# First two heads' queries from raw tokens, their mean and scale put in behind, in an attention and MLP kernel

## The chip, the cores and the metric

The kernel runs on one core of one Trainium2 chip. Its time is the device time of one execution in microseconds, given as the median of several runs. A profile is one execution recorded by the hardware profiler; its span runs from the first to the last instruction of the program and is a little shorter than the device time of the same execution.

## The reference

One layer with two branches over 2048 tokens of width 512. All inputs are bf16.

```python
x  = A_x                               # 1 x 2048 x 512
xn = layernorm(x)                      # no gain, no bias, eps 1e-5
# attention branch: 32 heads of width 128, keys and values from a cache of 2048 entries
q  = (xn @ wq) split into heads        # wq: 512 x 4096
p  = softmax(q k^T * 128**-0.5)
s  = (p v, heads joined) @ wo          # wo: 4096 x 512
# MLP branch on the same xn
h  = gelu(layernorm(xn) @ w1)
hs = four quarters of h, shifted by +1, -1, +2, -2 tokens, @ w2
x1 = xn + hs
g  = silu(x1 + gelu(layernorm(x1) @ w3) @ w4)
out = x + s * g
```

## The kernel before

The attention branch sets the order. Its work is cut into 128 units: 8 groups of 4 heads, in each group 4 tiles of 512 queries, for each tile the 4 heads. A unit has 8 slots. A slot `n` handles 256 of the 2048 keys: two 128x512 score matmuls into a pair of PSUM banks (`s_slot`, tile `ps_s`, of which there are two), one ScalarE exponential of 128x1024 into `pT`, and two value matmuls into `ps_o` (`pv_slot`) for a slot that lies some slots back. That distance is the lag: 5 at the start, raised by one at each slot number in `STEPS` until it is 12 from slot 158 on. There are 1024 slots. In between VectorE adds up the `pT` tiles (`add_first`, `add_next`, `fold`) for the softmax sums. The sums of the first four units are turned by small matmuls (`sums`), those of later ones by a DMA transposition; the reciprocals go through DRAM and come back on all partitions (`bcast`), and `norm` multiplies the unit's output with them.

The query of a unit (`q_mm`, `q_copy`) is four matmuls over `xnT`, the transposed normalized tokens, into a bank of the pool `psX`. This pool has two tags with one buffer each, "xa" and "xm". A tile with such a tag waits until the earlier tile of the tag has been read. Row sums, output projections (`wo_mm`) and the MLP's matmuls take these two banks as well.

All of it is one program written slot by slot in the loop over `n`. Each engine and each DMA queue (SP's, ACT's, POOL's) executes its own instructions strictly in the program's order; `pin` keeps that order. `at(n, fn)` puts a piece of work behind slot `n`; the table `tokens` holds, for the token tiles 4 to 15, the slots of their statistics, of their normalization and of the transposition into `xnT`. The MLP's chunks start in unit 5.

The start of the program stands ahead of slot 0. Four tiles of 128 tokens are loaded on the SP and ACT queues, the query weights of heads 0 to 3 on the POOL queue, keys (by transposing DMA, `load_k`, four pieces of 512 keys a head) and values (`load_v`, two halves a head) on the SP queue. TensorE does 48 matmuls of no use on the identity (`warm_up`). `first_stats` takes mean and variance of the four tiles (VectorE, one tile on ScalarE) and the factor (variance + eps) to the power -0.5 on GpSimd. `first_tokens` normalizes each tile on VectorE, transposes it by four matmuls with the identity, copies it to `xnT`, and makes head 0's query in pieces of 128 tokens. The queries of heads 1 to 3 follow in slots 1, 3 and 5 and are copied by VectorE in slots 2, 4 and 6.

Of the kernel before, what the change touches and what calls it, by code (L numbers as in the profile page):

```python
# [17 lines left out]
def kernel(  # L18
# [36 lines left out]
    LAG = 5  # L55
# [5 lines left out]
    WARM = 48  # L61
# [3 lines left out]
    def pool(name, bufs=1, space=None, **kw):  # L65
        if space is not None:
# [11 lines left out]
    nc.vector.memset(ones_t[:], 1.0)  # L78
    nc.vector.memset(nhalf[:], -0.5)
    ident = const.tile([P, P], BF16, name="ident")  # L80
    diag = const.tile([P, P], FP32, name="diag")
    pin(nc.gpsimd.iota(diag[:], pattern=[[-1, P]], base=0, channel_multiplier=1,
                       allow_small_or_imprecise_dtypes=True))
    pin(nc.vector.tensor_scalar(
        out=ident[:], in0=diag[:], scalar1=0.0, scalar2=None, op0=ALU.is_equal))
# [20 lines left out]

    xsrc = x2d.rearrange("(t p) d -> t p d", p=P)
    wq_v = A_wq.rearrange("(dc p) j -> p dc j", p=P)
# [34 lines left out]
    STEPS = (36, 40, 44, 48, 49, 150, 158)  # L143
    LAGS = [(n, LAG + i) for i, n in enumerate(STEPS)] + [(NS, LAG + len(STEPS))]
    kTs, vBs, wqs, wos, oTs, st = {}, {}, {}, {}, {}, {}
# [135 lines left out]
    def bcast(u):  # L281
        st[u]["rb"] = (tl["rb"].tile([P, 512], FP32, tag="rb3", bufs=2, name="rb") if u >= T1 else rp.tile([P, 512], FP32, name="rb"))
# [111 lines left out]
    def ln1_load(t, eng):  # L394
        xin = tokp.tile([P, D], BF16, tag="ta", bufs=6, name="xin")
# [10 lines left out]
    def first_stats():  # L406
        root = D ** -0.5
        nm = smp.tile([P, 1], FP32, name="nm")
        junk = gtp.tile([P, D], BF16, tag="pre", name="pre")
        pin(nc.scalar.activation(  # L410
            out=junk[:], in_=ln[3][:], func=ACT.Identity, scale=-root / D, accum_out=nm[:]))
        pin(nc.scalar.activation(
            out=junk[:], in_=ln[3][:], func=ACT.Square, scale=root, bias=nm[:],
            accum_out=mvA[:, 3, 1:2]))
        for t in range(3):
            bn = smp.tile([P, nc.vector.BN_STATS_DIM], FP32, name="bn")
            pin(nc.vector.bn_stats(out=bn[:], in_=ln[t][:]))
            pin(nc.vector.bn_aggr(out=mvA[:, t, :], in_=bn[:]))
        for a, b in ((0, 1), (1, 2), (2, 4)):
            ve = smp.tile([P, b - a], FP32, name="ve")  # L420
            pin(nc.gpsimd.tensor_scalar(
                out=ve[:], in0=mvA[:, a:b, 1], scalar1=EPS, scalar2=None, op0=ALU.add))
            pin(nc.gpsimd.tensor_tensor(
                out=rsA[:, a:b], in0=ve[:], in1=nhalf[:, 0:b - a], op=ALU.pow))
        return lambda: pin(nc.vector.tensor_scalar(
            out=mvA[:, 3, 0:1], in0=nm[:], scalar1=-1.0 / root, scalar2=None, op0=ALU.mult))

# [5 lines left out]
    def ln1_norm(t):  # L433
        xin = ln.pop(t)
        xn = ph1.tile([P, D], BF16, tag="xn", bufs=5, name="xn")
# [11 lines left out]
    def warm_up(n):  # L447
        wt = psS.tile([P, 2, 512], FP32, name="ps_s")
        for _ in range(n):
            mm(wt[:, 0, 0:P], ident[:], ident[:], True, True)  # L450

    def first_tokens():
        xns = [ln1_norm(t) for t in range(2)]
        mean_3()
        xns += [ln1_norm(t) for t in range(2, 4)]
# [552 lines left out]
```

## Time and profile before

| | us |
|---|---|
| median of 3 runs | 1249.34 (1248.23 to 1252.16) |
| the profiled execution | 1248.59 |
| its span | 1246.8 |
| TensorE matmul busy | 1239.2 (99%) |
| VectorE busy | 1115.2 (89%) |
| ScalarE busy | 1129.5 (91%) |
| GpSimd busy | 171.3 (14%) |
| first exponential starts | 10.67 |

A row of the timeline reads: start, length, engine (with a q: its queue issues a DMA), line, operation, output<-inputs by the program's names, shapes, how many instructions the row joins, and in brackets how long the engine had been idle and what ended that. A group of a tile's view gives shortest, median and longest duration in ns, and first and last start. A row of the waits gives who waited for whom, the sum in us, the number and the longest. A row of the windows gives a stretch, its length, then busy time and number of instructions of each engine that the view holds, granted TensorE clock, DMA share and GB/s. A matmul's length in a row contains its way through the array; how often one can start is read from the distance of starts. PE is TensorE, PEld its weight load, DVE VectorE, ACT ScalarE, POOL GpSimd, SP the queue that only issues DMAs.

### The profile page before, as it was taken

What the parts mean: (1) busy time and instruction counts of PE and PEld (TensorE: products, weight loads), DVE (VectorE), ACT (ScalarE), POOL (GpSimd) and SP (SyncE); (2) the same over time, 40 slices, a digit from 0 to 9 for tenths busy, and PEclk for the clock granted to TensorE, in tenths of its full rate; (3) what the DMA queues carried; (4) which work ended last, traced back from release to release, by engine and by line L of the source; (5) the groups of instructions that cost most, each with busy time, mean ns of one, the idle gap of its engine ahead of it and who ended that gap; (6) DMA issues with size and microseconds to landing.
All of it is one profiled execution on the core that took longest, in us unless ns stands there. A gap on an engine that the chain in (4) does not pass through costs nothing.

```text
span 1246.8 us, 16616 instructions
## 1 busy us (share of the span) xinstructions
PE 1239.2 (99%) x5808; PEld 596.4 (48%) x5808; DVE 1115.2 (89%) x1518; ACT 1129.5 (91%) x1285; POOL 171.3 (14%) x299
## 2 busy tenths in 40 slices
PE   8999999999999999999999999999999999999998
PEld 5444444444444444444444444444444444444444
DVE  7999999999899988899989889899888999888998
ACT  8999999888999888899998889998888999988992
POOL 5563003432111000000100000010000000000110
PEclk9999999999999999999999999999999999999999
DMA  9556473565734545243573345633345233653453
GB/s 198 126 111 104 88 154 77 129 130 114 153 67 101 114 98 120 55 88 73 108 155 85 68 76 106 136 79 83 81 105 119 56 89 66 130 136 77 106 149 106
DMA packets 248404, 131.42 MB, mean 105 GB/s; under 512 B 200000, under 2 KB 224960, under 8 KB 248320
## 3 DMA queue, kind: packets, MB, share of 16 engines
q1 hardware_dynamic: 238752, 103.94, 41.1%
q0 software_dynamic: 8992, 25.96, 8.0%
q8 instruction: 45, 0.74, 0.3%
q10 hardware_dynamic: 576, 0.46, 0.1%
q14 instruction: 39, 0.32, 0.1%
HBM read 83.62 MB, written 8.13 MB: 74 GB/s over the span
## 4 chain that ended last, share of the span: by engine, by line
PE 93%; DVE 3%; DMA 2%; ACT 1%; issue 0%; SPq 0%; DVEq 0%
PE ps_s L122 34%; PE ps_o L122 33%; PE ps_m L122 9%; PE ps_wo L122 8%; PE ps_q L122 8%; DMA rb<-dr 1%; DVE acc L224 1%; ACT pT L213 1%; DMA dr<-rc 0%; DVE acc L219 0%; DMA accT<-acc 0%; DVE qT L199 0%; DVE sm L266 0%; DVE acc L228 0%; DVE oT L293 0%
## 5 line engine op out<-in xcount | busy, mean ns | idle before, releaser
L213 ACT ACTIVATE pT<-ps_s 128x1024 bf16<-128x1024 f32 x1024 | 1022.1, 1029 | 90.7 <-PE ps_s L122 76.3
L122 PE MATMUL ps_s<-qT,kT 128*128 128x512 bf16 x2048 | 608.8, 379 | 0.8 <-ACT pT L213 0.5
L122 PE MATMUL ps_o<-pT,vb 128*128 128x512 bf16 x2048 | 607.4, 379 | 0.4 <-DVE oT L300 0.4
L122 PEld LDWEIGHTS <-kT 128*128 128x128 bf16 x2048 | 231.7, 113 | 228.8 <-issue 6.0
L224 DVE TENSOR_TENSOR acc<-acc,pT 128x2048 bf16<-128x2048 bf16 x256 | 308.9, 1207 | 7.3 <-ACT pT L213 6.6
L122 PEld LDWEIGHTS <-vb 128*128 128x128 bf16 x2048 | 200.2, 98 | 226.0 <-issue 0.7
L219 DVE TENSOR_TENSOR acc<-pT 128x2048 bf16<-128x2048 bf16 x128 | 156.2, 1221 | 30.9 <-ACT pT L213 30.5
L122 PE MATMUL ps_q<-xnT,wq_h 128*128 128x512 bf16 (+1 forms) x524 | 152.8, 374 | 0.6 <-ACT xnT L477 0.4
L293 DVE TENSOR_TENSOR oT<-ps_o,rb 128x512 bf16<-128x512 f32 x122 | 130.8, 1072 | 9.5 <-DMA rb<-dr 9.4
L122 PE MATMUL ps_wo<-wo_h,oT 128*128 128x512 bf16 (+1 forms) x460 | 135.1, 377 | 0.0
L379 DVE TENSOR_TENSOR s_acc<-ps_wo,s_acc 128x512 f32<-128x512 f32 x96 | 66.0, 688 | 42.6 <-PE ps_wo L122 42.4
L228 DVE TENSOR_TENSOR acc<-acc 128x1024 bf16<-128x1024 bf16 x128 | 87.5, 683 | 0.9
L266 DVE TENSOR_REDUCE sm<-accT 128x4 f32<-128x512 bf16 x122 | 83.0, 680 | 1.1 <-DMA accT<-acc 1.0
L199 DVE CAST qT<-ps_q 128x512 bf16<-128x512 f32 x109 | 75.0, 688 | 7.9 <-PE ps_q L122 6.9
L122 PEld LDWEIGHTS <-wq_h 128*128 128x128 bf16 x524 | 50.8, 98 | 60.8 <-issue 1.0
L122 PE MATMUL ps_m<-w_sb,h2T 128*128 128x512 bf16 x224 | 77.1, 379 | 0.5 <-DVE xr L700 0.5
L122 PE MATMUL ps_m<-xn2T,w_sb 128*128 128x512 bf16 x224 | 77.1, 379 | 0.0
L682 POOL DMA_DIRECT2D w_sb<-in_B_w_dram x28 | 21.2, 756 | 372.3 <-PE ps_m L122 325.3
L122 PEld LDWEIGHTS <-oT 128*128 128x128 bf16 x468 | 45.7, 98 | 54.1
L710 POOL DMA_DIRECT2D g_d<-xr x16 | 8.8, 548 | 438.3 <-DVE xr L708 438.3
L229 DVE TENSOR_TENSOR acc<-acc 128x512 bf16<-128x512 bf16 x128 | 54.4, 425 | 4.4
L514 DVE SCALAR_TENSOR_TENSOR sq<-sq,pre 128x1024 bf16<-128x1024 bf16 x36 | 44.0, 1222 | 4.7 <-ACT sq L510 4.6
(98 smaller groups left out, 627.9 us busy)
## 6 DMA issues: line engine op xcount, KB each, us to landing
rb<-dr SPq DMA_DIRECT2D x127, 256.0 KB, 3.9
vb<-in_A_v_cache_dram SPq DMA_DIRECT2D x60, 256.0 KB, 3.4
w_sb<-in_B_w_dram POOLq DMA_DIRECT2D x28, 256.0 KB, 3.6
wo_h<-in_A_wo_dram SPq DMA_DIRECT2D x32, 128.0 KB, 2.8
wq_h<-in_A_wq_dram SPq DMA_DIRECT2D x28, 128.0 KB, 2.9
kT<-in_A_k_cache_dram SPq DMA_TRANSPOSE x128, 3.4
dr<-rc SPq DMA_DIRECT2D x128, 2.0 KB, 1.7
xr<-in_A_x_dram POOLq DMA_DIRECT2D x16, 128.0 KB, 2.5
```

The costliest lines, as they stand in the source:

```text
L122: pin(nc.tensor.matmul(out=out, lhsT=lhsT, rhs=rhs, start=start, stop=stop))
L199: pin(nc.vector.tensor_copy(out=qT[:], in_=st[u].pop("psq")[:]))
L213: pin(nc.scalar.activation(out=s["pT"][-1][:, jj:jj + 2, :], in_=sps[:], func=ACT.Exp, scale=SCALE))
L219: pin(nc.vector.tensor_tensor(out=s["acc"][:], in0=s["pT"][0][:], in1=s["pT"][1][:], op=ALU.add))
L224: pin(nc.vector.tensor_tensor(out=a[:], in0=a[:], in1=st[u]["pT"][i][:], op=ALU.add))
L228: pin(nc.vector.tensor_tensor(out=a[:, 0:2, :], in0=a[:, 0:2, :], in1=a[:, 2:4, :], op=ALU.add))
L229: pin(nc.vector.tensor_tensor(out=a[:, 0, :], in0=a[:, 0, :], in1=a[:, 1, :], op=ALU.add))
L266: pin(nc.vector.tensor_reduce(out=sm[:], in_=s.pop("at")[:], axis=mybir.AxisListType.X, op=ALU.add))
L293: pin(nc.vector.tensor_tensor(out=oTs[(g, qt)][:, hh, :].rearrange(f, j=4), in0=s["o"].rearrange(f, j=4), in1=s["rb"].rearrange("x (p j) - ...
L379: pin(nc.vector.tensor_tensor(out=sa, in0=ps[:], in1=sa, op=ALU.add))
L514: pin(nc.vector.scalar_tensor_tensor(out=sq[:].rearrange(f2), in0=sq[:].rearrange(f2), scalar=1.0, in1=pre[:].rearrange(f2), op0=ALU.add, ...
L682: pin(nc.gpsimd.dma_start(out=w[:], in_=w3_v[:, :, fc * P:(fc + 2) * P]))
```

## The change

The query of heads 0 and 1 for the first 512 tokens no longer waits for normalized tokens. The raw tiles are transposed as they land, into `xT`. For head 0, two halves of 256 tokens each, and for head 1 all 512:

- `q_raw`: four matmuls of the query weights with `xT`;
- `q_mean`: one more matmul into the same bank that contracts over a single row, the column sums of the weights (`w_sum`, `w_copy`) with the row of negative token means (`means`, `m_copy`);
- `q_scale`: VectorE multiplies the bank with the tokens' factors, spread over the partitions by matmuls (`factors`; the factor is split into a bf16 part and a bf16 remainder, `high` and `low`) and copied to `rsb` by ScalarE (first half) and VectorE (second half).

Slots 0 and 1 are done in `first_tokens` in halves of 256 queries (`s_part`). The first 512 keys of head 0 are loaded as they are (`kx`, ACT queue), transposed by four matmuls (`k_turn`) and copied by VectorE (`k_back`). `xnT` of the first 512 tokens is made afterwards for heads 2, 3 and the MLP: VectorE adds the mean (`centred`), GpSimd multiplies by the factor (`scaled`), each in four pieces of 128x512. Queries 2 and 3 move to slots 9 and 10, and 13 and 14. The statistics of the first four tiles are all taken by VectorE, in two pairs, with two powers on GpSimd.

Around this: the query weights of heads 0 to 3 come in two loads of two heads; the x tiles 4 to 7 are loaded on SP's queue and normalized in place; the warm-up has 23 matmuls on a tile of constants and does not need the identity; the lag starts at 3; the table of token tiles, the loads of keys and values of heads 2 and 3 and of the output weights, and the slots of row sums, broadcasts and normalizations of the first units are moved; unit 2's value bank is "xm"; queries 5 and 6 are made in two slots with two matmuls each.

```diff
-    LAG = 5
+    LAG = 3
-    WARM = 48
+    WARM = 23
+    CENT, SCAL = (0, 0, 1, 1), (1, 1, 2, 2)
+    FA, FN = ((0, 1), (2,), (3,)), (1, 2)
+    QNEXT = ((2, 9), (3, 13))
...
-    STEPS = (36, 40, 44, 48, 49, 150, 158)
+    STEPS = (14, 25, 33, 41, 44, 48, 49, 150, 158)
...
-            st[u] = dict(psq=psX.tile([P, 512], FP32, tag="xm" if HG <= u < HG + 3 or u > QUIET + 1 else "xa", name="ps_q"))
+            st[u] = dict(psq=psX.tile([P, 512], FP32, tag="xm" if u in (2, 3) or u > QUIET + 1 else "xa", name="ps_q"))
...
-            s["o"] = psO.tile([P, 512], FP32, name="ps_o")
+            s["o"] = (psX.tile([P, 512], FP32, tag="xm", name="ps_o") if u == 2 else
+                      psO.tile([P, 512], FP32, name="ps_o"))
...
+    def q_raw(h, dcs, ps, cs=slice(0, 512), last=False):
+        for dc in dcs:
+            mm(ps[:, cs], wqs[h][:, dc, :], raw["xT"][:, dc, cs], dc == 0, last and dc == DC - 1)
+
+    def q_mean(h, ps, cs=slice(0, 512)):
+        mm(ps[:, cs], raw["ws"][:, h * P:(h + 1) * P], raw["nmb"][0:1, cs], False, True)
+
+    def q_scale(h, ps, rb, cs=slice(0, 512)):
...
+        pin(nc.vector.tensor_tensor(out=st[h]["qT"][:, cs], in0=ps, in1=rb, op=ALU.mult))
...
+        stats(0)
+        for t in range(2):
+            turn(t)
+            back(t)
         turn(2)
...
+        turn(3)
+        back(2)
+        stats(1)
+        means(0)
+        m_copy(0)
...
+        k_turn(kps)
+        w_sum(0, rps[0])
+        w_copy(0, rps[0])
+        back(3)
...
+        q_raw(0, range(DC), psq[0], H2[0])
+        factors(0)
...
+        q_mean(0, psq[0], H2[0])
+        means(1)
+        m_copy(1)
+        q_raw(0, range(DC), psq[1], H2[1])
+        k_back(kps[:])
...
+        q_scale(0, psq[0][:, H2[0]], rsb[:, H2[0]], H2[0])
+        q_mean(0, psq[1], H2[1])
...
+        s_part(0, H2[0])
+        high(1)
+        low(1)
...
+        s_part(1, H2[0])
+        factors(1)
+        q_scale(0, rps[1][:, H2[0]], qs[:], H2[1])
+        q_raw(1, FA[0], raw["ps"])
+        for p in range(2):
+            s_part(p, H2[1])
+        pin(nc.vector.tensor_copy(out=rsb[:, H2[1]], in_=rps[1][:, H2[0]]))
+
+    def centred(dc):
+        pin(nc.vector.tensor_tensor(
+            out=xnT[:, dc, 0:512], in0=raw["xT"][:, dc, :], in1=raw["nmb"][:], op=ALU.add))
+
+    def scaled(dc):
+        pin(nc.gpsimd.tensor_tensor(
+            out=xnT[:, dc, 0:512], in0=xnT[:, dc, 0:512], in1=raw["rb"][:], op=ALU.mult))
...
-    tokens = ((2, 4, 5), (5, 9, 11), (8, 12, 13), (11, 14, 14),
-              (21, 27, 27), (26, 31, 31), (33, 36, 36), (35, 39, 39),
-              (37, 45, 45), (47, 53, 53), (55, 61, 61), (63, 69, 69))
+    tokens = ((2, 5, 6), (4, 7, 8), (7, 11, 12), (9, 13, 14),
+              (16, 20, 20), (21, 25, 25), (29, 35, 35), (34, 38, 38),
+              (49, 55, 55), (55, 61, 61), (60, 66, 66), (65, 70, 70))
...
-        at(3 + i, lambda i=i: load_v(2, (i,), nc.gpsimd))
+        at(7 + i, lambda i=i: load_v(2, (i,), nc.gpsimd))
...
+    norms = {26: 0, 34: 1, 38: 2, 42: 3}
...
-        s_slot(u, p)
+        if n > 1:
+            s_slot(u, p)
...
-        if u == 0 and p in (1, 3, 5):
-            q_mm(1 + p // 2, range(DC))
-        if u == 0 and p in (2, 4, 6):
-            q_copy(p // 2)
+        if n in FN:
+            q_raw(1, FA[1 + FN.index(n)], raw["ps"])
+        if n == FN[-1]:
+            q_mean(1, raw["ps"])
+            q_scale(1, raw["ps"][:], raw["rb"][:])
+        for dc in range(DC):
+            if CENT[dc] == n:
+                centred(dc)
+            if SCAL[dc] == n:
+                scaled(dc)
+        for h, n0 in QNEXT:
+            if n in (n0, n0 + 1):
+                q_mm(h, (2 * (n - n0), 2 * (n - n0) + 1))
+            if n == n0 + 2:
+                q_copy(h)
```

More of the change, by code (lines that the diff above doesn't have):

```diff
@@ L77 @@
     rstd2 = const.tile([P, NT], FP32, name="rstd2")
[L78 to L85, printed above, removed]
     kp = ent(pool("kp", HG + 1))
@@ L404, in ln1_stats @@
         rsqrt(rs1[t][:], mv1[t][:, 1:2])
[L406 to L426, printed above, removed]
     def norm1(t, out, in_):
```

208 lines of the change are left out of this document (141 added, 67 removed).

## The prediction

> **What bounds the kernel now.** I read the page first (busy time, the chain that ended last), then the timeline of the first 40 us, the waits of the first 60 us, and single tiles.
>
> ```profile
> span 1246.8 us, 16616 instructions
> PE 93%; DVE 3%; DMA 2%; ACT 1%; issue 0%; SPq 0%; DVEq 0%
> 1.39 4.33 PE L122 MATMUL ps_s<-ident 128*128 128x128 bf16 x48 [1.39 <-DVE ident L84]
> 3.31 0.69 DVE L417 BATCH_NORM_STATS2 bn<-xin 128x6 f32<-128x512 bf16 x1 [1.98 <-DMA xin<-in_A_x_dram]
> 4.36 0.63 ACT L410 ACTIVATE pre<-xin 128x512 bf16<-128x512 bf16 x1 [1.21 <-DMA xin<-in_A_x_dram]
> 6.17 0.88 PE L122 MATMUL ps_o<-ident,xn 128*128 128x128 bf16 x8 [0.44 <-DVE xn L429]
> 10.04 1.03 PE L122 MATMUL ps_s<-qT,kT 128*128 128x512 bf16 x4 [0.36 <-ACT qT L499]
> 11.77 0.59 PE L122 MATMUL ps_s<-qT,kT 128*128 128x512 bf16 x2
> 16.85 14.77 ACT L213 ACTIVATE pT<-ps_s 128x1024 bf16<-128x1024 f32 x16 [0.33 <-PE ps_s L122]
> 17.95 0.59 PE L122 MATMUL ps_s<-qT,kT 128*128 128x512 bf16 x2
> 18.38 0.59 PE L122 MATMUL ps_o<-pT,vb 128*128 128x512 bf16 x2
> ```
>
> TensorE is the chain: 93%. The last two rows start 0.43 us apart for two matmuls, so one 512-wide matmul costs 0.2155 us; a slot (2 score, 2 value matmuls) costs TensorE 0.86 us. In the early slots ScalarE is just slower: (14.77 - 1.03)/15 = 0.916 us per exponential of 16. A slot with two query matmuls costs 6 x 0.2155 = 1.29 us. From slot 2 on (scores at 11.77) hardly any time is free, so a change ahead of it moves the end by what it moves that start, and every later wait of TensorE adds fully. What can be gained lies ahead of 10 us: the first x tile is there at 3.31, the last of four at 4.36, but the first useful matmul comes at 6.17 and the first scores at 10.04, because statistics, normalization, transposition and queries stand in a row. The profiled execution took 1248.59 us; my sum is made against that. The median of the runs shown is 1249.34, 0.75 higher.
>
> **The start, new.** The rows that price it:
>
> ```profile
> 4.04 0.18 DVE L418 BATCH_NORM_AGGREGATE mvA<-bn 128x2 f32<-128x6 f32 x1
> 4.14 0.66 DVE L417 BATCH_NORM_STATS2 bn<-xin 128x6 f32<-128x512 bf16 x1
> 6.34 0.82 POOL L423 TENSOR_TENSOR rsA<-ve,nhalf 128x2 f32<-128x2 f32 x1
> 6.60 1.09 ACT L477 ACTIVATE xnT<-ps_o 128x512 bf16<-128x512 f32 x2 [0.67 <-PE ps_o L122]
> 8.60 0.38 ACT L494 ACTIVATE qT<-ps_q 128x256 bf16<-128x256 f32 x1
> 14.16 0.69 DVE L199 CAST qT<-ps_q 128x512 bf16<-128x512 f32 x1 [0.64 <-PE ps_q L122]
> L300 DVE TENSOR_TENSOR oT<-ps_o,rb x7: 415/684/692, 30.1 to 1235.4; 128x512 bf16<-128x512 f32 x5, 128x256 bf16<-128x256 f32 x2
> DMA to landing us min/median/max: 4.4/5.3/6.3
> DMA to landing us min/median/max: 4.0/5.7/7.9
> ```
>
> Raw tiles go to TensorE as they land, behind 23 warm-up matmuls (about 1.1 to 3.5 us). ScalarE's four evictions (1.09/2 each) end near 7.1 with the small copies among them. VectorE sets the pace: four statistics of 0.69 from 3.31, some eleven small ones about 0.10 apart, the key eviction of 0.69: 7.85. The factor of the first half (power of 0.82 on GpSimd, hidden behind the second pair of statistics) goes through TensorE and a ScalarE copy of 0.38 and is ready near 7.9. So the first scaled query half takes 7.95 to 8.37 (0.415), the first half scores start at 8.45, the second half is scaled by 9.72, and the four half exponentials (about 0.5 each, from the 0.54 of a 512-wide activation) run from 8.95 to 11.2. Slot 2 needs the PSUM pair of the third of them, which ends near 10.7: its scores start at 10.75, not 11.77: **-1.02**.
>
> The change adds 24 matmuls of 128 columns, 2 of 256 and 1 of 512 to TensorE, 4096 columns, 8 x 0.2155 = 1.7 us. All but the last query matmul of head 1 and its mean row fit into waits ahead of 10.75. Those two are still owed: **+0.43**.
>
> Queues. POOL issues two pairs of wq, the first ahead of the index tile; the identity comes near 2.2, and is first needed at 3.5 (if that cover failed, the same delay would reach the transposes). The wq landing times (4.4 to 6.3 us, first of the two landing rows) put the first pair at 5.3 to 7.1; it is needed near 6.5: I take 0, and 0.5 if late. ACT's queue gets one issue for the raw keys while ScalarE waits for tiles: 0. SP loses one transposing load, gets four x tiles from POOL and sends the first values earlier (near 4.2; by the second landing row, 4.0 to 7.9, there at 8.2 to 12.1). First use is slot 3 at 12.0: 0, at worst 0.1. The 25 dropped warm-ups lay in front of work that waited anyway: 0, unless the clock suffers (below). The shorter lag moves value matmuls forward without changing their number, and by slot 158 both kernels have the same lag: 0.
>
> **What the new work does to VectorE and GpSimd.** The normalized tokens are still needed for heads 2 and 3: four 128x512 sums on VectorE (`centred`) and four 128x512 products on GpSimd (`scaled`). Behind those on POOL stands the factor of token tile 4, and VectorE, in order, waits for it before it applies tile 4. Behind that instruction on VectorE stand the sums of exponentials, statistics of tiles 6 and 7, and then the copy of query 2 that frees the bank "xm". TensorE's query 3 in slot 13 waits for that copy.
>
> ```profile
> 12.60 0.69 DVE L402 BATCH_NORM_STATS2 bn<-xin 128x6 f32<-128x512 bf16 x1
> 13.33 0.18 DVE L403 BATCH_NORM_AGGREGATE mv<-bn 128x2 f32<-128x6 f32 x1
> 13.61 0.22 POOL L126 TENSOR_SCALAR ve<-mv 128x1 f32<-128x1 f32 x1 [2.08 <-DVE mv L403]
> 13.91 0.57 POOL L127 TENSOR_TENSOR rs<-ve,nhalf 128x1 f32<-128x1 f32 x1
> 14.76 1.22 DVE L219 TENSOR_TENSOR acc<-pT 128x2048 bf16<-128x2048 bf16 x1
> 15.90 0.41 DVE L429 TENSOR_SCALAR xn<-xin,mv,rs 128x512 bf16<-128x512 bf16 x1
> 20.19 0.69 DVE L228 TENSOR_TENSOR acc<-acc 128x1024 bf16<-128x1024 bf16 x1
> 20.92 0.43 DVE L229 TENSOR_TENSOR acc<-acc 128x512 bf16<-128x512 bf16 x1
> 22.38 0.18 DVE L251 RECIPROCAL rc<-ps_sum 128x4 f32<-128x4 f32 x1
> 23.27 1.19 DVE L219 TENSOR_TENSOR acc<-pT 128x2048 bf16<-128x2048 bf16 x1
> 23.44 1.10 POOL L126 TENSOR_SCALAR ve<-mv 128x1 f32<-128x1 f32 x1 [0.25 <-DVE mv L403]
> L132 POOL TENSOR_TENSOR vn<-vn,rsA 128x1 f32<-128x1 f32 x4 | 0.9, 235 | 0.3
> PE ps_o L122 <- DVE oT L300: 0.4, 1, 0.4
> PE ps_s L122 <- ACT pT L213: 0.3, 1, 0.3
> ```
>
> No wide GpSimd arithmetic is in this trace. Low end of one product: 0.43, VectorE's own 128x512 sum. I take 0.9: VectorE's 128x512 product with an fp32 factor (0.684) and the 0.2 that a GpSimd product of one column costs; it is the nearest row in kind and size. High end: the row at 23.44 took 1.10 instead of 0.22 because a VectorE sum of two tiles ran from 23.27 to 24.46, so each product may lose another 0.88: 1.78.
>
> VectorE: second half scaled at 9.72, factor copy 10.1, four sums of 0.43 to 11.8, query 1 scaled to 12.5, statistics of tile 4 to 13.4, first sum of exponentials. GpSimd: two products 11.8 to 13.6; the sum of exponentials (1.22) comes in between to 14.85; two more to 16.65; factor of tile 4 (0.22 + 0.57 and gaps, 0.9) to 17.55. VectorE resumes at 17.6: apply 0.41, sum 1.22, apply 0.41, statistics 0.9, sum 1.22, folds 1.15, statistics 0.9, copy 0.69: 6.9, so query 2 is copied at 24.5. TensorE: slot 2 ends 10.75 + 0.86 = 11.61; six slots of 0.916 to 17.1; slots 9 and 10 with 1.29 to 19.7; two more to 21.5; scores and values of slot 13 to 22.4. Query 3 waits from 22.4 to 24.5: **+2.1**. From that copy to the copy of query 4 VectorE has 12.0 us (five sums 6.1, folds 1.15, three applications 1.23, two reciprocals 0.36, two statistics 1.8, two copies 1.38): 36.5. TensorE gets to query 5, which needs that bank, in slot 24 at 24.5 + 0.56 (half a query, row sums) + 0.86 (slot 14) + 7 x 0.916 + 0.13 (row sums) + 2.58 (slots 22 and 23) + 0.86 = 35.9: **+0.6**. GpSimd products themselves end at 16.65, ahead of query 2's second half in slot 10 (near 19): 0. The key loads and transposes behind SP's waits are due with at least a microsecond left. The later normalization of head 0 (slot 26) is due for a value bank in slot 29 with 0.2 us left: 0.
>
> Two waits of before, the 0.4 for a value bank and the 0.3 in the last two rows, stand at places that the change rebuilds (head 2's values go to "xm"; slot 3 starts otherwise): **-0.7**.
>
> Sum: -1.02 + 0.43 + 2.1 + 0.6 - 0.7 = +1.4. Forecast **1250.0 us** (0.1% above the profiled execution, 0.05% above the median).
>
> The Trainium skill, GPSIMD Engine Reference, section 3.1, gives a two-input elementwise operation there 2.6 cycles per element at 1.2 GHz; an estimate from that page is 512 x 2.6 / 1.2 = 1.11 us, so the sum by the page would be 4 x 0.2 = 0.8 higher, 1250.8. The Trainium skill, SBUF — State Buffer, section "Who interferes with whom", says that VectorE instructions with two SBUF inputs and GpSimd instructions that read SBUF lock each other out for a whole instruction; the 1.10 at 23.44 agrees.
>
> **Rivals.**
> Faster: GpSimd keeps up. At 0.43 a product the factor of tile 4 is ready at 14.4, VectorE gets to its application at 15.5 unhindered, query 2 is copied at 22.4, and the first stall is gone: 1.4 - 2.1 = -0.7, 1247.9; with 0.6 more if the second goes too, 1247.3. For it: the lead of 1 us is worked out from plain rows. Against it: VectorE has no slack left even so.
> Slower: products at the high end. 4 x 0.88 = 3.5 more in front of tile 4's factor, all of it on query 3: 1253.5. It decides (past 0.3%, 3.75 us) from about 1.5 us a product. For it: four sums of VectorE and one of 1.22 want the same tiles at that time.
> Clock: a slower PE start.
>
> ```profile
> 1.39:4.39 3.00, 3.00 (x29) 3.00 (x30) 0.00 (x0) 1.00 0.85 243
> 4.50:5.70 1.20, 1.20 (x21) 1.05 (x18) 0.00 (x0) 1.00 0.99 90
> ```
>
> The 128-wide warm-ups (windows on the identity's tile; second column TensorE) run 29 in 3.00 us at first, 21 in 1.20 later: 0.107 against 0.055 us, with the granted clock at 1.00 in both. After, useful work of about 46 such widths meets the start. If the change of pace comes one such stretch of 3 us later, that is 46 x 0.05 = 2.3 us, of which half lies in waits, and some half-paced scores: +1.5 to +2, 1251.8. The Trainium skill, TensorE: Matmul & The Clock Gate, Part 1, says that the window which decides is free-running; by that rule a shorter warm-up could meet it or not from run to run.
> The change may also not do what it says, if x lands later beside the raw keys: the start stays and the stalls stay, 1251.
>
> **Chances.** Forecast case 0.36 (its own range 1248.6 to 1251.6), faster rival 0.22 (down to 1245 with waits that I do not see), slower rival 0.30, clock 0.09, the last 0.03. 0.3% (3.75 us) is about what a measurement of this kernel can tell from no change. Below 1245.6: 0.08, a third of the faster rival and little else, since even a start without any wait gains hardly 3 us. Above 1253.1: 0.30, most of the slower rival and a part of the clock's. Range 1246.3 to 1254.5.
>
> **What would show it.** Scores of slot 2 near 10.75; a wait of TensorE at a `ps_q` matmul for VectorE's `qT` near 22 of about 2 us, and one near 36; VectorE idle near 15 to 17.6 until GpSimd's factor of tile 4; GpSimd products of 0.9 with longer ones beside VectorE's sums. The prediction is wrong if products take under 0.6 or over 1.5, or if half-paced matmuls reach past 6 us.

## The result, and the profile after

| | before | after |
|---|---|---|
| median of 22 runs each, us | 1251.34 (1248.23 to 1257.58) | 1257.03 (1252.91 to 1260.89) |
| ratio, 95% interval | | 1.0043 (1.0034 to 1.0053) |
| profiled execution, us | 1248.59 | 1255.14 |
| its span, us | 1246.8 | 1253.4 |
| exponential of slot 2 starts | 12.50 | 16.33 |
| of slot 13 / 14 | 23.22 / 24.13 | 27.20 / 30.06 |
| of slot 40 | 50.17 | 56.44 |
| of slot 1023 | 1223.92 | 1230.19 |

The kernel became slower by 0.43%, some 5.4 us; 1250.0 was forecast, with a range up to 1254.5. The last rows of the table are the starts of ScalarE's exponentials, read slot by slot from the two traces, one execution of each kernel. Their difference is the ledger used below: +3.83 us at slot 2, +6.27 at slot 40, +6.26 at the last slot. All that is left at the end arises in the first 56 us. Between slots 40 and 1023 two small steps (+0.70 at slot 69, -0.67 between slots 512 and 768) cancel.

From the page of the changed kernel, its span:

```profile
span 1253.4 us, 16625 instructions
```

From its timeline, TensorE's rows:

```profile
4.68 1.00 PE L138 MATMUL ps_s<-ident,xin 128*128 128x128 bf16 x8
...
8.04 0.40 PE L138 MATMUL ps_k<-ident,kx 128*128 128x128 bf16 x4 [2.10 <-DMA kx<-in_A_k_cache_dram]
8.37 0.38 PE L138 MATMUL ps_r<-wq,mean 128*1 128x128 bf16 x4
...
10.43 1.06 PE L138 MATMUL ps_q<-xT,wq 128*128 128x256 bf16 x4
...
15.70 0.59 PE L138 MATMUL ps_s<-qT,kT 128*128 128x512 bf16 x2
...
28.87 0.59 PE L138 MATMUL ps_q<-xnT,wq 128*128 128x512 bf16 x2 [1.38 <-DVE qT L215]
...
38.77 0.59 PE L138 MATMUL ps_q<-xnT,wq 128*128 128x512 bf16 x2 [1.04 <-DVE rc L268]
```

Three things are to be seen. TensorE stands still for 2.10 us ahead of 8.04, because the four key transposes come first in its order and the raw keys land at 8.00. The transposes themselves are still at full pace, but from 8.93 to 15.7 the matmuls go at half pace: four of 256 columns take 1.06 at 10.43; at full pace they take 0.60 (next section). So slot 2's scores start at 15.70, where 10.75 was forecast and 11.77 had been. And TensorE waits for VectorE at query 3 (28.87) and at a query in slot 22 (38.77), there for a bank that VectorE's reciprocal has to free.

The same timeline, VectorE's rows and one of GpSimd:

```profile
8.48 1.30 DVE L458 CAST kT<-ps_k 128x512 bf16<-128x512 f32 x1 [1.19 <-PE ps_k L138]
...
14.51 3.36 DVE L597 TENSOR_TENSOR xnT<-xT,nmb 128x512 bf16<-128x512 bf16 x4
...
15.09 4.93 POOL L601 TENSOR_TENSOR xnT<-xnT,rsb 128x512 bf16<-128x512 bf16 x4 [5.68 <-DVE xnT L597]
...
19.21 1.89 DVE L235 TENSOR_TENSOR acc<-pT 128x2048 bf16<-128x2048 bf16 x1
...
21.88 0.41 DVE L427 TENSOR_SCALAR xin<-xin,mv,rs 128x512 bf16<-128x512 bf16 x1
...
23.89 0.41 DVE L427 TENSOR_SCALAR xin<-xin,mv,rs 128x512 bf16<-128x512 bf16 x1 [0.47 <-POOL rs L143]
...
28.16 0.66 DVE L215 CAST qT<-ps_q 128x512 bf16<-128x512 f32 x1
...
38.22 0.41 DVE L427 TENSOR_SCALAR xn<-xin,mv,rs 128x512 bf16<-128x512 bf16 x1 [0.78 <-POOL rs L143]
38.55 0.18 DVE L268 RECIPROCAL rc<-ps_sum 128x4 f32<-128x4 f32 x1
```

The wait for GpSimd's factor of tile 4, which the forecast made 2.75 us (14.85 to 17.6), does not occur: tile 4 is normalized at 21.88 without a wait, and only tile 5, at 23.89, waits 0.47 for its factor. VectorE is simply busy, for 12.97 of the 13.65 us from 14.51 to the copy of query 2 at 28.16: the four sums took 3.36 instead of 1.7, the first sum of exponentials 1.89 instead of 1.22.

### The profile page after: what moved, and what is told of

Read it like the earlier page. It is cut to its first block, busy times and chain, and to the rows that moved or that the text cites. A ratio compares the mean times of both kernels' runs of the same rounds, so it can differ in the third digit from the quotient of the medians.

```text
span 1253.4 us, 16625 instructions
## 1 busy us (share of the span) xinstructions
PE 1243.3 (99%) x5806; PEld 597.5 (48%) x5806; DVE 1120.6 (89%) x1530; ACT 1128.8 (90%) x1288; POOL 173.4 (14%) x293
## 4 chain that ended last, share of the span: by engine, by line
PE 93%; DVE 4%; ACT 1%; DMA 1%; POOL 1%; issue 1%; ACTq 0%; SPq 0%; DVEq 0%; POOLq 0%
PE ps_s L138 33%; PE ps_o L138 33%; PE ps_m L138 10%; PE ps_q L138 8%; PE ps_wo L138 8%; ACT pT L229 1%; DVE acc L240 1%; DMA kx<-in_A_k_cache_dram 1%; DVE bn L422 0%; DVE acc L235 0%; DMA rb<-dr 0%; POOL rs L143 0%; POOL ve L142 0%; DVE xnT L597 0%; DVE acc L244 0%
## 5 line engine op out<-in xcount | busy, mean ns | idle before, releaser
L138 PE MATMUL ps_s<-qT,kT 128*128 128x512 bf16 (+1 forms) x2052 | 610.0, 379 | 0.2 <-ACT pT L229 0.2
L138 PE MATMUL ps_q<-xnT,wq_h 128*128 128x512 bf16 x448 | 133.2, 379 | 0.0
L138 PEld LDWEIGHTS <-wq_h 128*128 128x128 bf16 x448 | 43.8, 98 | 52.8
```

The costliest lines, as they stand in the source:

```text
L138: pin(nc.tensor.matmul(out=out, lhsT=lhsT, rhs=rhs, start=start, stop=stop))
```

## The experiments

All times "at slot n" are starts of that slot's exponential; "against before" is their difference to the profile of the kernel before. Each run was timed beside the kernel before on one chip; its ratio is to that. Edits are shown against the changed kernel unless the text says otherwise.

**Keys by transposing DMA.**

```diff
-    raw["kx"] = tokp.tile(...); pin(nc.scalar.dma_start(out=raw["kx"][:], ...))
-    load_k(0, (1, 2))
+    load_k(0, (0, 1, 2))
...
-        k_turn(kps)
-        k_back(kps[:])
```

> Edit: the first 512 keys of head 0 come by transposing DMA again, as in the kernel before; the raw keys, their four transposes on TensorE and their eviction are gone; the rest of the change stays. Theory A (the raw keys, landed at 8.00, hold TensorE up from 5.7 to 8.0, and the pause lowers the clock afterwards): no wait of TensorE between 5.7 and 8, granted clock 1.00 throughout, first exponential of slot 2 near 12.5 instead of 16.33, time about 4 us below the changed kernel's 1257.0. Rival B (the 25 dropped warm-ups lower the clock): the clock falls to 0.5 all the same, slot 2 at 14.5 to 15.5, 1 to 2 us below. Rival C (x and weights are late by themselves, by 0.5 and at 6.78): slot 2 at 15.5 or later, under 1 us below. All expect the wait at query 3 to stay.

Measured: 1253.81, ratio 1.0014 (1.0000 to 1.0027). Its timeline, TensorE:

```profile
7.17 0.38 PE L138 MATMUL ps_r<-wq,mean 128*1 128x128 bf16 x4 [1.40 <-DMA wq<-in_A_wq_dram]
7.49 0.61 PE L138 MATMUL ps_q<-xT,wq 128*128 128x256 bf16 x4
...
12.18 0.59 PE L138 MATMUL ps_s<-qT,kT 128*128 128x512 bf16 x2 [0.25 <-ACT pT L548]
```

Slot 2's scores come at 12.18 instead of 15.70, with 23 warm-ups and full pace (0.61 for four of 256 columns). B and C, as far as they concern slot 2, fall. A is borne out as a whole (slot 2 at 12.81, 12.5 expected), but this run doesn't separate the wait from the half pace. TensorE now waits 1.40 for the weights: the late keys had hidden that they are late too.

**Queries ahead of the key transposes.**

```diff
-        k_turn(kps)
         w_sum(0, rps[0])
...
         q_raw(0, range(DC), psq[1], H2[1])
+        k_turn(kps)
         k_back(kps[:])
```

> Edit: on TensorE the four key transposes are moved behind the column sums and the first two raw query halves, so only they, and no longer the queries, wait for the raw keys; no load is moved. Theory A (the pause of 2.3 us, then half pace): work of TensorE begins at the landing of the weights near 6.8 instead of at 8.0, the pause shrinks to about 1 us; if that is too short to lower the clock, slot 2 comes near 13 and the time is about 3 us below 1257.0; if it still lowers it, slot 2 near 15 and 1 us below. Rival B (warm-ups): clock 0.5 all the same, slot 2 near 15. Rival C (the weights are late): slot 2 near 15.5, under 1 us below.

Measured: 1256.22, ratio 1.0031 (1.0013 to 1.0049); slot 2 at 17.09. It tells little: in this profile weights and raw keys landed at 8.39 and 9.88 instead of 6.78 and 8.00. Over the eight profiles that load the raw keys behind the same loads, their landing ranges from 6.74 to 9.88 and that of the weights from 6.46 to 8.39. So starts of different runs are compared below by what follows the landing.

**Filling the pause.**

```diff
         kps = psO.tile([P, 512], FP32, tag="ps_o", name="ps_k")
+        warm_up(36, psX.tile([P, P], FP32, tag="xm", name="ps_w"))
         k_turn(kps)
```

> Edit: 36 more matmuls of no use on the identity, just ahead of the key transposes on TensorE, so that it is not idle while it waits for the raw keys; the wait for them stays. Theory A with the clock as a consequence of the pause: granted clock 1.00 from 8 to 16 us, 128-wide matmuls of 0.055 instead of 0.107, slot 2 near 14 instead of 16.33, time about 2 us below 1257.0. If the clock's fall has another cause than the pause, it falls all the same and slot 2 stays near 16.3, the time within 0.5 us. If the wait itself was the whole loss, slot 2 also stays near 16.3, but at clock 1.00.

Measured: 1257.15, ratio 1.0039 (1.0020 to 1.0057). TensorE:

```profile
5.92 2.70 PE L138 MATMUL ps_w<-mean 128*128 128x128 bf16 x36
8.98 0.40 PE L138 MATMUL ps_k<-ident,kx 128*128 128x128 bf16 x4 [0.35 <-DMA kx<-in_A_k_cache_dram]
...
10.72 0.60 PE L138 MATMUL ps_q<-xT,wq 128*128 128x256 bf16 x4
...
14.31 0.59 PE L138 MATMUL ps_s<-qT,kT 128*128 128x512 bf16 x2 [0.25 <-ACT pT L548]
```

The keys landed 0.9 later than in the changed kernel, and yet slot 2's scores come 1.4 earlier: 5.33 us behind the first key transpose instead of 7.66. The half pace, and with it 2.3 us, is the pause's. The median did not fall, though 2 us less was expected. In this profile 4.4 us are lost at slots 541 to 560, where the changed kernel's had no such loss:

```profile
659.50 1.06 DVE L312 TENSOR_TENSOR oT<-ps_o,rb 128x512 bf16<-128x512 f32 x1 [4.52 <-DMA rb<-dr]
...
683.34 0.58 PE L138 MATMUL ps_m<-w_sb,h2T 128*128 128x512 bf16 x1 [2.70 <-DVE xr L803]
```

VectorE waits 4.52 there for a broadcast of reciprocals, against 1.67 in the changed kernel's profile, and TensorE then waits for VectorE. The next run loses 3.9 at slots 525 to 559, with 5.00 for that broadcast. Why it came late in these two isn't shown. So the 2.3 us are shown at the start of one profile, and not in the median.

**48 warm-ups again.**

```diff
-    WARM = 23
+    WARM = 48
```

> Edit: 48 matmuls of no use at the start, as in the kernel before, instead of 23; nothing else. Theory A (the pause of TensorE until the raw keys land lowers the pace afterwards): full pace is reached near 4.5, the pause ahead of the key transposes stays at 1.5 us or more, matmuls at half pace (128 wide 0.107, 256 wide 0.21) follow it for some us, and slot 2 comes 7 us or more behind the landing of the raw keys (8.3 behind it in the changed kernel; 6.0 behind it where the pause was filled); time 1256 to 1258. Rival B (the dropped warm-ups are the cause): full pace throughout, slot 2 about 6 us behind that landing, time about 2 us below 1257.0.

Measured: 1260.08, ratio 1.0074 (1.0053 to 1.0095). TensorE:

```profile
1.04 4.18 PE L138 MATMUL ps_w<-mean 128*128 128x128 bf16 x48 [1.04 <-DVE nhalf L105]
...
8.98 0.40 PE L138 MATMUL ps_k<-ident,kx 128*128 128x128 bf16 x4 [2.75 <-DMA kx<-in_A_k_cache_dram]
...
10.75 1.06 PE L138 MATMUL ps_q<-xT,wq 128*128 128x256 bf16 x4
...
15.73 0.59 PE L138 MATMUL ps_s<-qT,kT 128*128 128x512 bf16 x2 [0.25 <-ACT pT L548]
```

Full pace came at 3.9 here, a pause of 2.75 followed, and the matmuls are at half pace again from 10.75; slot 2 comes 7.4 us behind the landing at 8.94. Rival B, the forecast's clock rival in its own form (too few warm-ups), falls: it is the pause.

**Smaller first load of weights.** Against the run with transposed keys:

```diff
-    load_pair(0)
+    load_one(0)
     ...
-    load_pair(2)
+    load_one(1)
...
+    load_pair(2)
     load_v(1, (0, 1), nc.gpsimd)
```

> Edit: keys by transposing DMA as in the run before that did this, and besides the weights of heads 0 and 1 come in two loads of 128 KB instead of one of 256 KB, with the pair of heads 2 and 3 issued behind the first tokens. Theory G (what was left of the loss at the start, slot 2 at 12.81 instead of the 11.5 that the forecast amounts to, is the landing of the larger weights load at 7.13, TensorE idle for 1.40): the first weights land near 6 (5.74 for 128 KB in the kernel before), no wait over 0.4 for them, slot 2 at 11.4 to 11.9, time about 1 us below that run's 1253.8. Rival H (statistics, factor and copies set the pace, the weights only cover them): slot 2 at 12.3 or later. Granted clock 1.00 in both, if a pause of 1.4 us didn't lower it and a shorter one doesn't.

Measured: 1253.45, ratio 1.0020 (1.0009 to 1.0032). TensorE:

```profile
6.16 0.38 PE L144 MATMUL ps_r<-wq,mean 128*1 128x128 bf16 x4 [0.31 <-DMA wq<-in_A_wq_dram]
...
11.17 0.59 PE L144 MATMUL ps_s<-qT,kT 128*128 128x512 bf16 x2 [0.25 <-ACT pT L554]
...
17.86 0.62 PE L144 MATMUL ps_s<-qT,kT 128*128 128x512 bf16 x2 [1.04 <-DMA kT<-in_A_k_cache_dram]
```

The weights landed at 6.12, slot 2's scores start at 11.17: G holds, and with these loads the new start comes within 0.4 us of the forecast's 10.75, though without the raw keys' transposes and eviction, which the forecast had in it. It is 0.5 to 1.3 ahead of before at slots 2 to 7, and then loses 1.1 at slot 8 (head 1's keys, now behind more loads; the last row), 1.1 at slot 13 and 1.2 at slot 22. So a start 4.5 us earlier than the changed kernel's ends in 3 us at slot 1023.

**Query 3 later.**

```diff
-    QNEXT = ((2, 9), (3, 13))
+    QNEXT = ((2, 9), (3, 16))
```

> Edit: query 3 is issued at slot 16 instead of 13; nothing else is moved. Theory A (the loss at slot 13, exponential of slot 14 2.86 us behind that of slot 13, is TensorE's in-order wait for VectorE's copy of query 2): the step from slot 13 to 14 goes back to about 0.95, no wait at query 3 in slot 16 or one under 0.5, and the 2 us are gone at slot 40 too, time 2 us below 1257.0. Rival D (VectorE is in arrears altogether, and some later wait takes its place, for the row sums or query 5): the step at slot 14 goes, but the same 2 us come back by slot 40, time within 0.7 us. The start (slot 2 at 16.33) stays in both.

Measured: 1257.55, ratio 1.0052 (1.0033 to 1.0071). Its waits in the first 60 us:

```profile
PE ps_o L138 <- DVE qT L215: 1.9, 1, 1.9
```

The step at slot 14 is gone (0.91 instead of 2.86), but 1.9 stand at slot 21, where head 2's values want the bank that the copy of query 3 frees. From slot 9 to 40 the run loses 2.5 against before, the changed kernel 3.0. VectorE goes from the copy of query 2 at 28.87 to that of query 3 at 36.55 with one pause of 0.68. Rival D holds: VectorE is in arrears, and the wait moves.

**Products on VectorE; products left out.**

```diff
     def scaled(dc):
-        pin(nc.gpsimd.tensor_tensor(
+        pin(nc.vector.tensor_tensor(
```

> Edit: the four products run on VectorE instead of GpSimd; nothing else. Without GpSimd's reads beside them the four sums should take 1.7 instead of 3.36 and the first sum of exponentials 1.22 instead of 1.89; the products add 4 x 0.43 to 4 x 0.69, 1.7 to 2.8. Theory D (mutual holding-up, and the sum of VectorE's work, decide): VectorE 0.6 us earlier to 0.5 later at the copy of query 2, the step at slot 13 stays between 1.8 and 3.4 (2.86 now), time within 1 us of 1257.0. Rival F (VectorE waits in its order for GpSimd's late factor of token tile 4, as predicted): the factor is early, the wait at query 3 goes below 0.5, time 1.5 to 2 us below.

```diff
-            if SCAL[dc] == n:
-                scaled(dc)
```

> Edit: the four products on GpSimd are left out, so heads 2 and 3 (and the MLP) read the first 512 tokens centred but not multiplied with their factor. Theory D (VectorE has too much to do ahead of the copy of query 2, the four sums and what GpSimd makes slower): without GpSimd's products the sums take 1.7 instead of 3.36 and the first sum of exponentials 1.22 instead of 1.89, VectorE is 2.3 us earlier, and the step from slot 13 to 14 falls from 2.86 to 0.9 to 1.3; the loss between slots 9 and 40 against the kernel before falls from 3.0 to about 1 us. Rival J (the copy of query 2 is late because it stands behind the statistics of tiles 6 and 7 and their GpSimd factors, whatever ahead of it is faster): the step stays over 2 us.

Measured: 1255.62, ratio 1.0036 (1.0023 to 1.0049), and 1256.43, 1.0035 (1.0019 to 1.0051). The operations on the tile `xnT`, in the first case (min, median, max in ns):

```profile
L597 DVE TENSOR_TENSOR xnT<-xT,nmb x4: 414/420/423, 12.7 to 14.9; 128x512 bf16<-128x512 bf16 x4
L601 DVE TENSOR_TENSOR xnT<-xnT,rsb x4: 683/684/687, 13.3 to 16.4; 128x512 bf16<-128x512 bf16 x4
```

and in the changed kernel:

```profile
L597 DVE TENSOR_TENSOR xnT<-xT,nmb x4: 415/900/1389, 14.5 to 16.5; 128x512 bf16<-128x512 bf16 x4
```

With GpSimd idle each sum takes 0.42, so its products had doubled them. The Trainium skill, SBUF — State Buffer, section "Who interferes with whom", has an operation of VectorE with two SBUF inputs contend with a GpSimd instruction that reads SBUF; these two rows agree. But the products cost VectorE as much when it does them itself: from the first sum to the copy of query 2 it takes 13.4 us (12.68 to 26.09), against 13.65 in the changed kernel, and the step at slot 14 stays at 2.91. From slot 9 to 40 this run loses 3.05 against before, the changed kernel 3.00. F falls. Without products (heads 2 and 3 and the MLP then read tokens without their factor) the stretch is 12.6 (15.66 to 28.28), 1.0 less and not the 2.3 expected, since VectorE then waits 1.34 for TensorE's query of head 1; the step falls to 1.42 and the loss from slot 9 to 40 to 1.55, nearer to what D expects (0.9 to 1.3, and about 1) than to J's step of over 2. In these two runs it is the amount of work ahead of that copy, not the engine of the products, that counts. Neither time differs clearly from the changed kernel's.

**Tokens normalized and turned by DMA.**

```diff
-                centred(dc)
+                ln1_apply(dc)
...
-                scaled(dc)
+                ln1_turn(dc)
```

> Edit: the four sums (centred) on VectorE and the four products (scaled) on GpSimd are replaced by what the other token tiles get: each of the first four tiles is normalized by one VectorE operation of 128x512 and turned by a transposing DMA, at the same slots. Theory D (VectorE is in arrears because the sums and the GpSimd products hold each other up: sums 3.36 for four instead of about 1.7, first sum of exponentials 1.89 instead of 1.22): VectorE is 2.4 us earlier (4 x 0.41 for 3.36, and 0.67), query 2 is copied before TensorE needs the bank, the step from slot 13 to 14 is 0.9 instead of 2.86, the wait in slot 22 is under 0.5, time 2 to 3 us below 1257.0. Rival E (VectorE's usual work in slots 2 to 13, with two more statistics ahead of that copy, is the arrears): a wait of over 1 us at query 3 stays and the time falls by less than 1 us. The start (slot 2 near 16 to 17) stays in both.

Measured: 1257.55, ratio 1.0046 (1.0031 to 1.0060). The step at slot 14 falls to 1.33 and no more time is lost at slot 22, which is nearer to D than to E; but the time did not fall by D's 2 to 3 us, and TensorE, 1.8 us later than in the changed kernel already at slot 9, left VectorE more time. The four transposes are issued from 19.0 on, behind other loads on SP's queue, so TensorE waits 1.3 for them at query 2 in slot 9; the keys had landed 1.1 later, too. The windows of this run show something else:

```profile
12.00:14.00 2.00, 2.00 (x13) 1.02 (x13) 0.66 (x3) 0.75 (x3) 0.00 (x0) 1.00 1.09 359
```

and its timeline, in that window:

```profile
12.13 1.06 PE L138 MATMUL ps_q<-xT,wq 128*128 128x256 bf16 x4
```

The granted clock is given as 1.00, the matmuls go at half pace. In this run the column doesn't show the slowness.

**All three together** (transposed keys, smaller loads, tokens turned by DMA).

> Edit: all three mended parts together: keys by transposing DMA, weights of heads 0 and 1 in two loads, tokens of heads 2 and 3 normalized on VectorE and turned by DMA. If G and D hold: slot 2 at 11.4 to 11.9, step from slot 13 to 14 of 0.9, no wait of TensorE over 0.5 us up to slot 40, time 1249.5 to 1251, ratio to the kernel before 0.998 to 1.000. If E holds, a wait of 1 to 2 us stays at query 3 and the time is 1252 or more.

Measured: 1262.45, ratio 1.0084 (1.0069 to 1.0100). Its waits:

```profile
PE ps_q L144 <- DMA xnT<-xn: 10.4, 1, 10.4
PE ps_s L144 <- DMA kT<-in_A_k_cache_dram: 1.3, 1, 1.3
```

A clear miss. The start is right (slot 2 at 11.87), but the token transposes leave SP's queue at 20.6, behind six transposing loads of keys, and TensorE stands for 10.4 us. When that queue would be free for them had not been counted.

**Other slots for the token tiles, and query 2 copied by ScalarE.** Both have transposed keys, smaller loads, head 1's keys ahead of token tiles 4 to 7, its values on SP's queue, and the table `tokens` of the kernel before (but for tile 4, normalized and turned one slot later); the second adds

```diff
-        if u > QUIET + 1 or mlp.get("stage") == 2:
+        if u == 2 or u > QUIET + 1 or mlp.get("stage") == 2:
```

> Edit: start as in the run with transposed keys and two loads of weights; besides, head 1's keys are issued piece by piece ahead of token tiles 4 to 7, head 1's values behind them on the same queue, and the statistics and normalizations of token tiles 4 to 15 stand in the slots of the kernel before. Sums and products of the first tokens stay as in the changed kernel. Expected by theories G and D: slot 2 at 11.6 to 12.0 and 0.7 to 1.3 ahead of the kernel before up to slot 9, no wait for head 1's keys at slot 8 (1.04 in that run), step at slot 13 of 1.0 to 1.9 (one statistic of 0.87 less and 0.4 less ahead of the copy), the 0.7 at slot 69 gone, time 1250.0 to 1251.5, ratio 0.999 to 1.001. If VectorE's arrears do not depend on that table, the time is 1252 to 1253.

> Edit: as the run beside it, and query 2 is copied by ScalarE instead of VectorE. Expected: no wait of TensorE at query 3, step at slot 13 of 0.9 to 1.0; ScalarE, which sets the pace in these slots with 0.916 an exponential against TensorE's 0.86, loses about 0.6 once at slot 11; time 0.3 lower to 0.5 higher than the run beside it. If VectorE's arrears only move on, TensorE waits for it later (row sums, query 5) and nothing is won.

Measured: 1252.64, ratio 1.0024 (1.0015 to 1.0033), and 1252.71, 1.0018 (1.0008 to 1.0027). The second loses nothing at slot 14 (0.0 to 0.1 behind before from slot 12 to 21), the first 1.9. Yet both reach slot 23 at the same time, 34.55 and 34.56 (before: 33.17): what the copy gained is lost again in slot 22. There the second waits for token tile 7, turned by a DMA, and not for VectorE's reciprocal, which had started at 31.53:

```profile
33.50 0.59 PE L144 MATMUL ps_q<-xnT,wq 128*128 128x512 bf16 x2 [1.57 <-DMA xnT<-xin]
```

Both lose another 1.7 to 1.9 near slot 46.

**The changed kernel's table, then token tile 8 to 15 later.** Transposed keys, smaller loads, head 1's values on SP's queue, query 2 copied by ScalarE; tile 15 two slots later. The second run then takes the slots of tiles 8 to 15 from the kernel before:

```diff
-              (16, 20, 20), (21, 25, 25), (29, 35, 35), (34, 38, 38),
-              (49, 55, 55), (55, 61, 61), (60, 66, 66), (67, 72, 72))
+              (21, 27, 27), (26, 31, 31), (33, 36, 36), (35, 39, 39),
+              (37, 45, 45), (47, 53, 53), (55, 61, 61), (63, 69, 69))
```

> Edit: the changed kernel with four parts mended: keys of the first 512 by transposing DMA; weights of heads 0 and 1 in two loads, those of heads 2 and 3 behind the first tokens; head 1's values on SP's queue behind its keys; query 2 copied by ScalarE. The table of token tiles is the changed kernel's, but for tile 15 (statistics at slot 67, normalization at 72). Sums and products of the first tokens stay. Expected by the places measured so far: slot 2 at 11.8 to 12.0; 1.1 ahead of the kernel before at slot 9; 0.4 lost at slots 10 and 11 more than before, 0.5 at slot 11 for ScalarE's copy, so even at slot 13 and at slot 21; no wait of 1.6 for the turned tile 7 in slot 22 (the table of that run is left); the 1.9 at slots 40 to 50 of that run and the 0.7 at slot 69 gone: -0.5 to +0.5 at slot 96, time 1249.8 to 1250.8, ratio 0.999 to 1.001. If VectorE's arrears only come out later, 1.0 at query 4 or 5 in slots 22 to 24 as in the changed kernel: ratio 1.001 to 1.002.

> Edit: the run before (four parts mended) with the token tiles 8 to 15 in the slots of the kernel before, so that the statistics and normalization of tile 8 and its wait for GpSimd's factor (0.87 + 0.4 + 0.78, 2.05 us) stand behind VectorE's second reciprocal instead of ahead of it. Theory K (VectorE's work sets slot 23): the reciprocal comes 1.5 to 2 us earlier than 33.4, the wait of 2.0 at the query in slot 22 falls under 0.5, slot 23 comes near 33 instead of 34.7, and slot 40 lies 0.3 to 0.9 ahead of the kernel before; up to 1.7 may come back near slot 46, where these slots cost that in an earlier variant. Time 1249.3 to 1251. If the waits are independent, slot 23 stays at 34.5 or later.

Measured: 1253.80, ratio 1.0028 (1.0016 to 1.0040), and 1252.26, 1.0010 (0.9998 to 1.0022). TensorE's rows for slot 2 and for the query in slot 22 in the first:

```profile
10.88 0.59 PE L144 MATMUL ps_s<-qT,kT 128*128 128x512 bf16 x2 [0.25 <-ACT pT L554]
...
33.64 0.59 PE L144 MATMUL ps_q<-xnT,wq 128*128 128x512 bf16 x2 [2.03 <-DVE rc L274]
```

ScalarE's row for slot 23 in the first, and in the second:

```profile
34.70 1.02 ACT L235 ACTIVATE pT<-ps_s 128x1024 bf16<-128x1024 f32 x1 [2.46 <-PE ps_s L144]
```

```profile
33.11 1.02 ACT L235 ACTIVATE pT<-ps_s 128x1024 bf16<-128x1024 f32 x1 [0.47 <-PE ps_s L144]
```

The first has nearly the start that was forecast (scores of slot 2 at 10.88 for 10.75, their exponential at 11.51, 0.99 ahead of before) and no loss at slot 14, and still comes to slot 23 at 34.70. The two variants above came there within 0.15 us of it, but waited for tile 7; this one waits 2.03 for the reciprocal. Taking tile 8's statistics, normalization and wait from ahead of the reciprocal brings it from 33.41 to 31.82 and gives 1.6 us at slot 23, though the second run had started 0.40 later: K holds. How busy VectorE is from the first landed tile to its second reciprocal, by windows of the kernel before, of the changed one, and of these two (second number: busy, with the instructions):

```profile
3.30:30.68 27.38, 21.11 (x40) 1.00 1.02 208
```

```profile
3.30:38.55 35.25, 27.86 (x55) 0.90 0.75 163
```

```profile
3.30:33.41 30.11, 26.25 (x52) 1.00 0.95 186
```

```profile
3.30:31.82 28.52, 25.05 (x49) 1.00 0.97 191
```

The change puts 6.75 us more work on VectorE ahead of that instruction. Before, VectorE had 6.27 us of idle time there (27.38 - 21.11); with the start mended it has 3.5 to 3.9. Part of the work is only longer, not more: the four sums alone take 3.35 to 3.36 in these three kernels with the change, and 1.42 in the run without products. The last variant can't be told from the kernel before by its time; none beats it.

## Why the prediction was wrong, by its own steps

| place | forecast | measured, against before |
|---|---|---|
| slot 2 | -1.02 | +3.83 |
| slots 2 to 9: owed matmuls, a wait for `pT`, queries 2 and 3 gone from slots 3 and 5 | +0.43, -0.3 | -0.56 |
| slots 9 to 13, query 2's matmuls in their new place | in the times of the stall, not in the sum | +0.70 |
| slots 13 to 14, query 3 | +2.1 | +1.96 |
| slots 14 to 22, a wait for a value bank | -0.4 | -0.47 |
| slots 22 to 25 | +0.6 | +1.42 |
| slots 25 to 40 | 0 | -0.61 |
| slots 40 to 69 | 0 | +0.68 |
| behind slot 69 | 0 | -0.69 |
| sum | +1.4 | +6.26 |

The step that failed is "ACT's queue gets one issue for the raw keys while ScalarE waits for tiles: 0". The issue was counted, the landing was not. It took 6.34 us (1.66 to 8.00), TensorE was through with all work ahead of it at 5.94, and `k_turn` stands in TensorE's order ahead of everything that the raw tokens had made ready. The row for it was at hand: landings of 4.4 to 6.3 for the weights, taken for a load of 128 KB; and the pair of 256 KB, for which 5.3 to 7.1 was taken, landed at 6.78 here and at 6.46 to 8.39 elsewhere.

The size of this step has two parts. Slot 2's scores come 5.33 us behind the first key transpose where the pace stays full; with the transpose at 8.04 that makes 13.37. Without raw keys and with the smaller load of weights slot 2's scores came at 10.88 and 11.17. So raw keys and late loads cost 2.2 to 2.5 (0.3 of it the key transposes themselves), and the half pace after the pause the 2.33 from 13.37 to 15.70. In three runs at full pace the scores of slot 2 start 5.01 behind the first column sum (7.17 to 12.18, 6.16 to 11.17, 9.30 to 14.31), which itself starts as soon as keys or weights let it; in the last two variants, with weights landed at 4.97 and 5.14, it is 5.43. So for 10.75 the weights were needed by 5.7, not near 6.5 as the forecast has it.

The second part was among the rivals, with a chance of 0.09, +1.8 instead of 2.3, and a wrong cause. With 23 warm-ups full pace came at 5.42 instead of 3.9, but the half pace that cost time came with 48 as well; the pause brought it. Half-paced matmuls past 6 us were among the forecast's own signs of being wrong. The Trainium skill, TensorE: Matmul & The Clock Gate, Part 1, gives as the state of an idle array half the clock, after at least one idle window of about 3.4 us. Here the measurements differ: pauses of 2.10 and 2.75 were enough, and one of 1.27 as well (products on VectorE):

```profile
6.78 0.40 PE L138 MATMUL ps_k<-ident,kx 128*128 128x128 bf16 x4 [1.27 <-DMA kx<-in_A_k_cache_dram]
7.11 0.52 PE L138 MATMUL ps_r<-wq,mean 128*1 128x128 bf16 x4
7.56 1.03 PE L138 MATMUL ps_q<-xT,wq 128*128 128x256 bf16 x4
```

while the 1.40 of the run with transposed keys left the pace full. What decides between these two, no run here shows.

The stall at query 3 came at its place and nearly with its size: the slot took 1.96 more, for a forecast of 2.1, and 1.38 of that is the wait; query 3's own two matmuls, which the term did not hold, are in the rest. VectorE was given 14.4 us (10.1 to 24.5) from the first sum to the copy of query 2 and took 13.65. That these agree is luck, since the parts were wrong. The wait of 2.75 for tile 4's factor did not occur. The products took 1.23 each instead of 0.9 and their price fell on VectorE, in doubled sums and a longer sum of exponentials. The slower rival (products over 1.5 decide) therefore did not occur, though the result lies on its side.

"+0.6" at query 5 was too small, and its place another: TensorE waits at the first query of unit 4, in slot 22, for the reciprocal. The forecast listed VectorE's work between two copies, but missed that the new table moves tile 8's statistics from slot 21 to 16 and its normalization from 27 to 20, ahead of that reciprocal. The table was in the diff. The 0.70 at slot 69 (TensorE waits 0.5 for a query copy there) was missed in the same way; that it, too, comes from the table is likely, as neither the runs with the old table nor the one with tile 15 two slots later have it.

The term for the new start, -1.02, was never measured with raw keys on time. In the six runs with transposed keys and smaller loads slot 2 came 0.53 to 0.99 ahead of before; that the best of them meets the forecast is in part luck, as they have no key eviction on VectorE, which took 1.30 where the forecast counts 0.69. Of the -0.7 for two waits, the 0.4 for a value bank was there (in slot 22). The 0.3 was worth nothing, since the step at that slot was 0.90, ScalarE's pace. The owed matmuls cost 0.18 at slot 3 instead of 0.43. That slots 2 to 9 still gain 0.56 comes from queries 2 and 3, which had stretched the steps behind slots 3 and 5 to 1.18 and 1.34 (0.70 together over the usual pace). The sum of the forecast has no term for that, nor for the 0.70 that query 2 costs in its new place; the two happen to cancel. The rival that x lands later beside the raw keys shows only in little: the first statistics start at 3.83 instead of 3.31, and at 3.39 to 3.80 in runs without raw keys.

The remark against the faster rival, that VectorE has no slack left, was right. It was not carried to its end: where VectorE sets the time of slot 23, an earlier start of TensorE is waited away, as in the run that started 0.99 ahead of before and came to slot 23 1.53 behind it.

## What to carry to other kernels

A load that is moved is priced by when it lands against when its first reader's turn comes in that engine's order, not by what its issue costs; a reader that stands ahead of ready work holds it all up. When a change moves work to an engine that later has to free a buffer in time, add up that engine's busy time to that point, before and after (here 21.11 and 27.86 us): if its idle time doesn't cover the difference, waits will come out somewhere, and here taking one away moved it to the next place. Two variants that lose the same time at the same slot need not wait for the same thing: read the wait in each. Read the pace of TensorE from distances of starts of equal matmuls, and expect that a pause of 2 us ahead of a burst can cost a burst at half pace.

## What the runs showed of the hardware that was not expected

- A pause of TensorE of 2.1 to 3.1 us (six profiles), and once of 1.27, was followed by matmuls of half pace (256 columns 0.21 instead of 0.11) for 3 to 9 us, also where it had been at full pace since 3.9. One of 1.40 was not.
- The windows give a granted clock of 1.00 for a stretch at half pace in one run, and 0.50 in others.
- The same loads, issued at the same time, landed up to 3 us apart from run to run: the raw keys at 6.74 to 9.88.
- The key eviction, whose write is strided, took 1.30 us for 128x512; evictions of that size with a plain write took 0.69. That the stride is the cause is not shown by a run of its own.
- GpSimd's 128x512 product took 1.23 us (four in 4.93), against 0.684 on VectorE, and VectorE's sums beside it took up to 1.39 instead of 0.42.
